# Moving two of five convolution blocks per unit from TensorE to the other engines, with three engines sharing their taps

## The chip, the cores and the metric

One NeuronCore of one Trainium2 chip runs the whole kernel. The metric is the device time of one execution in microseconds; the median of three runs is given. A profile of one execution shows where the time of the engines goes.

## The reference, cut to what matters

The input is `x` of 8 sequences of 4096 tokens with 192 channels, as one list of 32768 tokens. Each of 8 heads (24 channels each) has 7 taps, made positive and normalised by a softmax. A causal convolution along the tokens is followed by two matrix products with an activation between them:

```python
w = softmax(weight)                                     # 8 heads x 7 taps
out[b, s, h] = sum_k w[h, k] * x_pad[b, s + k, h]       # 6 zeros ahead of each sequence
h = out @ w_in                                          # 192 -> 2048
g = h * cos(h)
return g @ w_out                                        # 2048 -> 192
```

## The kernel before, in words

The 32768 tokens are cut into 32 **units** of 1024 tokens. A unit is two **tiles** of 512 tokens; the loop runs over 64 tiles. I call the first tile of a unit the even tile and the second the odd tile.

A tile has eight **h steps** (`mm1`, lines 488 to 504). Step h*j* makes 256 of the 2048 hidden features for 512 tokens with six matmuls, in three pairs: the two matmuls of a pair use the upper and lower 64 rows of the array at once. The result takes two PSUM banks; three such double banks are used in turn, so step j+3 cannot begin before step j has been read out. ScalarE makes `cs = cos(h)` (a Sin, line 510), VectorE multiplies `g = h * cs` (line 514). The second product (`mm2_step`, line 552) of the tile before is spread between the h steps: 64 pairs of matmuls with 192 columns a tile. In the orders, `m9` means nine such pairs. VectorE and ScalarE copy one half of the result each (line 571).

In the middle of a tile's second product the halves of the array change places (`q`). To be sure that no two row halves write one bank at once, the class `Turn` lets a no-operation on SyncE (line 196) wait for the last matmuls ahead of the change, and lets the first matmul after it wait for that no-operation. The convolution does the same between its two halves `c1` and `c2`. SyncE works its queue strictly in order, and all transfers of the steady part are issued from the same queue.

From unit 4 on (`FIRST_RAW`) the convolution is done in two ways. A **conv block** of 112 tokens is done on TensorE with a band matrix (`conv_unit`, line 277: 16 matmuls, eight pairs, for all conv blocks of a unit together), copied by ScalarE into `ct_buf` (line 294) and turned by a transposing DMA (`X` and `x`, line 317). A **raw block** is turned first (`T`, line 345: `rT` holds channels on the partitions and tokens along the row), and its seven taps are multiplied and summed there. ScalarE makes the products of three taps into `pa` (line 356), in two halves of 348 elements; GpSimd makes the other four in one instruction of 2784 elements (line 363), adds the three of ScalarE and sums the rest in three adds (lines 370, 374, 377), giving `ro`. Four DMAs per unit (`U`, line 387) spread `ro` into `cT`, from where `mm1` reads. GpSimd also casts the loaded unit to bfloat16 (`K`, line 211).

The order of everything is written out by hand. `PE_ORDER` has one string for the even and one for the odd tile; it holds TensorE's steps and the points at which the steps of other queues are put into their queues. `ACT_ORDER` gives what ScalarE and VectorE do after the steps: `s3` is cos and product of step h3, `a211` a tap product (tap 2, half 1, put after h1), `Q` and `P` the two copies, `ec2` and `ec1` the copies of the convolution. `K+3` casts the unit three ahead, `L+4` loads the one four ahead, `T+3` turns the raw blocks of the unit three ahead, `R+1` is GpSimd's convolution for the next unit, `U+0` spreads the raw result of the unit at hand, `O` stores.

Before the change a unit has five conv blocks (560 tokens) and four raw blocks of 116 tokens. The even tile's 512 tokens come from conv blocks alone.

Of the kernel before, what the change touches and what calls it, by code (L numbers as in the profile page):

```python
# [16 lines left out]
def kernel(  # L17
# [14 lines left out]
    T = 512  # L32
# [26 lines left out]
    xf = x.rearrange("b s d -> (b s) d")  # L59

# [7 lines left out]
    rT_pool = ctx.enter_context(tc.tile_pool(name="rT", bufs=3))  # L68
# [21 lines left out]
    def load_unit(u, n0=0, n1=UB, queue=nc.sync):  # L90
        if u >= FIRST_RAW:
            x_tiles[u] = xin.tile([128, UB + 1, D], FP32, name="x_f")

            raw = NPB * OP + OR - 128
            for n0, n1, t0, step in ((NPB, NPB + 2, raw, 2 * OR), (NPB + 2, UB + 1, raw + OR, 2 * OR), (0, NPB, OP - 128, OP)):
                rows = xf[u * U + t0 : u * U + t0 + 128, :]
                rows = bass.AP(rows.tensor, rows.offset, [[D, 128], [step * D, n1 - n0], [1, D]])
                queue.dma_start(out=x_tiles[u][:, n0:n1, :], in_=rows)
# [74 lines left out]
    ct_bufs = [consts.tile([128, 2 * NC * NPB + 1, 64], BF16, name="ct_buf%d" % i) for i in range(2)]  # L173
# [95 lines left out]
    def conv_unit(u, banks):  # L269


        ps = banks()
        sides = [slice(0, 64), slice(64, 128)]

        def mm(h, side):
            first, last = h % 4 == 0 and h // 4 == side, h % 4 == 3 and h // 4 != side
            return nc.tensor.matmul(  # L277
                out=ps[h // 4][0:OP, 0 : NPB * 4 * G].rearrange("p (m i r) -> p i m r", m=NC * NPB, i=4)[:, h % 4],
                lhsT=band[sides[side], h, 128 - OP : 128], rhs=xk[u][sides[side], 0 : NC * NPB, R * h : R * (h + 1)],
                start=first, stop=last, skip_group_check=True)  # L280

        for h in range(4):
            ms = mm(h, 0), mm(h + 4, 1)
        turn = Turn()
        turn.mark(*ms)
        yield
        for h in range(4):
            ms = mm(h + 4, 0), mm(h, 1)
            if h == 0:
                turn.wait(*ms)  # L290
        yield
        for b in range(2):
            w0 = 4 * R * b
            nc.scalar.copy(ct_bufs[u % 2][0:OP, 0 : 2 * NC * NPB].rearrange("p (k n) m -> p k n m", k=NC)[:, :, 1 : NPB + 1, w0 : w0 + 4 * R],  # L294
                           ps[b][0:OP, 0 : NPB * 4 * G].rearrange("p (k n w) -> p k n w", k=NC, w=4 * R))
            if b:
                have.update((("conv", u, 0), ("conv", u, 1)))
            yield
# [10 lines left out]
    def turn_unit(u, n0=0, n1=UB + 1, part=0):  # L309
        if u >= FIRST_RAW:  # L310
            assert {("conv", u, 0), ("conv", u, 1)} <= have
            if part == 0:
                cT[u] = cT_pool.tile([128, NC * (UB + 1) * 128], BF16, name="cT")
            else:
                have.update((("whole", u, 0), ("whole", u, 1)))
            to = cT[u][:, 0 : NC * CW].rearrange("p (n s t) -> p s n t", s=2, t=OP)
            nc.sync.dma_start_transpose(out=to[:, part],
                                        in_=ct_bufs[u % 2][0:OP, part : part + 2 * NC * NPB].rearrange("p s m -> p (s m)"))
# [33 lines left out]
    def taps(u, j, half, mul):  # L352
        if u not in pa:
            pa[u] = pa_pool.tile([128, PA, WN, OR], FP32, name="pa")
        part = slice(HALF * half, HALF * (half + 1))
        mul(pa[u][:, j, part], tap_window(u, j)[:, part], tap[:, j : j + 1])  # L356

    raw_prod = consts.tile([128, K - PA, WN, OR], FP32)

    def conv_raw(u):  # L360

        a, p = pa.pop(u), raw_prod
        nc.gpsimd.tensor_tensor(out=p, in0=tap_window(u, PA, K),  # L363
                                in1=tap[:, PA:K].rearrange("p (j a b) -> p j a b", a=1, b=1).to_broadcast([128, K - PA, WN, OR]),
                                op=ALU.mult)
        add = nc.gpsimd.tensor_tensor
        n, done = K - PA, 0
        while done < PA:
            m = min(n, PA - done)
            add(out=p[:, 0:m], in0=p[:, 0:m], in1=a[:, done : done + m], op=ALU.add)  # L370
            done += m
        while n > 2:
            m = n // 2
            add(out=p[:, 0:m], in0=p[:, 0:m], in1=p[:, n - m : n], op=ALU.add)  # L374
            n -= m
        ro[u] = ro_pool.tile([128, WN, OR], BF16, name="ro")
        add(out=ro[u], in0=p[:, 0], in1=p[:, 1], op=ALU.add)  # L377

    def spread_raw(u):

        have.add(("raw", u))
        r = ro.pop(u).rearrange("p (k w) t -> p k (w t)", k=NC)
        for to, t0 in ((0, NPB * OP + OP), (1, NPB * OP)):
            d = cT[u][64 * to : 64 * to + 64, t0 : t0 + (NC - 1) * CW + NRB * OR]
            d = bass.AP(d.tensor, d.offset, [d.ap[0], [CW, NC], [2 * OR, 2], [1, 2 * OR]])
            for v in range(2):
                nc.sync.dma_start(out=d[:, :, v], in_=r[64 * v : 64 * v + 64])

    def mend_edges(u):

# [97 lines left out]
    def mm1(t, j, n0=0, n1=NB):  # L488

        assert ("whole", t // TPU, t % TPU) in have  # L490
        assert t < TPU * FIRST_RAW or t % TPU == 0 or ("raw", t // TPU) in have
        c = cT[t // TPU]
        h = h_pool.tile([128, 2, T], FP32, name="h")
        for k in range(NC):
# [97 lines left out]
    PE_FIRST = ["K1 h0a h0b W0 h1 h2 h3 r h4 w5 d11 w4 h5 d21 W1 c11 X0 m1 h6 m11 h7 L2 c21 D1",  # L592
# [19 lines left out]
    for t in range(NT + 1):  # L612
# [13 lines left out]
        def flush():  # L626
            while act:
# [8 lines left out]
                if k in "PQA":  # L636
                    if 0 <= made < NT - 1:
                        evac(made, int(k != "P"), nc.scalar.copy if k == "A" else None)
                elif k[0] in "ab":
                    if u + 2 in rT:  # L640
                        taps(u + 2, int(k[1]), int(k[2]), nc.scalar.mul if k[0] == "a" else nc.vector.tensor_scalar_mul)
                elif k[0] == "e":
                    next(conv[part_of(k[1:])], None)
                elif k[0] == "s" and t < NT:
                    gcu(t, int(k[1]), h[k[1:2] if k[2:] in "lr" else k[1:]], *HALVES[k[2:]])

        def of_unit(k, v):
# [7 lines left out]
            elif k == "L":  # L655
                load_unit(v)
                if v < FIRST_RAW:
                    load_edges(v)
            else:
                {"K": cast_unit, "D": double_unit, "X": turn_unit, "Y": mend_edges, "T": turn_raw, "R": conv_raw,  # L660
                 "U": spread_raw, "x": lambda u: turn_unit(u, part=1)}[k](v)

        for k in pe.split():
# [22 lines left out]
            elif k[1:] and k[1] != "+":  # L686
                of_unit(k[0], int(k[1]))
            else:
                if u + int(k[2:]) < NU and (k[0] not in "RUx" or u + int(k[2:]) >= FIRST_RAW):
                    of_unit(k[0], u + int(k[2:]))  # L690
            done.add(k)
            flush()
# [33 lines left out]
```

## Time and profile before

| | us |
|---|---|
| median of three runs (705.02 to 705.48) | 705.17 |
| span of the profiled execution | 703.5 |
| what a run has beside that span (705.17 less 703.5) | 1.7 |
| TensorE busy | 697.0 |
| VectorE busy | 642.4 |
| ScalarE busy | 644.4 |
| GpSimd busy | 503.7 |

The profile gives no time of its own for the profiled execution beside its span, so the span is set against the median of the runs. Busy times are unions of instruction spans. Matmuls are pipelined: their recorded spans overlap, and the pace of TensorE is read from the distance between starts. The clock granted to TensorE is 1.00 in every stretch of the steady part. In the rows, L followed by a number is a line of the kernel, `x16` a count, and a time in brackets is idle time with what ended it.

### The profile page before, as it was taken

The page shows a single profiled execution, that of the slowest core. Times are in us where ns is not written, and L with a number is a line of the kernel's source. Part 1 is how long each engine was busy: PE and PEld are TensorE (multiplying, and loading weights), DVE is VectorE, ACT ScalarE, POOL GpSimd, SP SyncE. Part 2 cuts the span into 40 slices and gives each one's busy share as a digit, 9 for nine tenths or more (in the row PEclk, how much of TensorE's full clock was granted, in tenths as well). Part 3 has the DMA queues.
Part 4 walks back from the last instruction along what each step waited for, and adds up shares of the span by engine and source line. Part 5 has one row for each costly group of instructions (what it writes and reads, how often), then busy time and mean ns, then how long its engine had stood idle before and what let it go on. Part 6 is the DMA issues. An engine that isn't in the chain of part 4 may idle for free.

```text
span 703.5 us, 26826 instructions
## 1 busy us (share of the span) xinstructions
PE 697.0 (99%) x11830; PEld 512.8 (73%) x11830; DVE 642.4 (91%) x598; ACT 644.4 (92%) x831; POOL 503.7 (72%) x214
## 2 busy tenths in 40 slices
PE   8999999999999999999999999999999999999997
PEld 4677777777777777777777777777777777777776
DVE  6889999999999999999999999999999999999996
ACT  7889999999999999999999999999999999999875
POOL 6524478977778877778877688877789778799400
PEclk9999999999999999999999999999999999999999
DMA  8964456667667768676656577577665576874331
GB/s 214 234 167 97 120 135 143 138 147 164 138 153 146 131 145 176 134 152 131 147 152 153 150 159 129 140 161 150 143 147 132 145 174 137 153 127 95 92 91 47
DMA packets 228292, 100.09 MB, mean 142 GB/s; under 512 B 156240, under 2 KB 227792, under 8 KB 228176
## 3 DMA queue, kind: packets, MB, share of 16 engines
q1 hardware_dynamic: 227464, 97.40, 62.7%
q8 instruction: 92, 1.51, 0.9%
q0 software_dynamic: 416, 0.79, 0.7%
q14 instruction: 24, 0.20, 0.1%
q10 hardware_dynamic: 296, 0.20, 0.1%
HBM read 31.36 MB, written 25.17 MB: 80 GB/s over the span
## 4 chain that ended last, share of the span: by engine, by line
PE 96%; DMA 1%; DVE 1%; POOL 0%; SPq 0%; ACT 0%; issue 0%; POOLq 0%
PE o_ps L552 48%; PE h L503 46%; PE h L277 2%; DMA wo_f<-in_moe_w_out_dram 1%; PE h L552 0%; SPq L124 0%; PE h L229 0%; DVE band L415 0%; POOL wo L120 0%; POOL mask L159 0%; DVE ct L438 0%; PE o_ps L432 0%; ACT mask L164 0%; DVE diag L404 0%; DVE prod L401 0%
## 5 line engine op out<-in xcount | busy, mean ns | idle before, releaser
L514 DVE TENSOR_TENSOR g<-h,cs 128x1024 bf16<-128x1024 f32 (+1 forms) x513 | 604.9, 1216 | 27.9 <-ACT cs L510 24.5
L510 ACT ACTIVATE cs<-h 128x1024 bf16<-128x1024 f32 (+1 forms) x513 | 511.0, 1021 | 44.0 <-PE h L503 30.6
L552 PEld LDWEIGHTS <-g 64*128 64x128 bf16 x8192 | 354.2, 94 | 102.2 <-issue 1.0
L552 PE MATMUL o_ps<-wo,g 64*128 64x192 bf16 x8128 | 420.6, 243 | 0.1
L503 PE MATMUL h<-cT,w 64*128 64x512 bf16 (+1 forms) x3078 | 407.0, 376 | 0.8 <-DVE g L514 0.4
L503 PEld LDWEIGHTS <-w 64*128 64x128 bf16 x3078 | 147.6, 94 | 75.0 <-issue 1.8
L211 POOL CAST xk<-x_f 128x768 bf16<-128x768 f32 (+1 forms) x56 | 76.4, 1367 | 113.9 <-DMA x_f<-in_x_dram 109.3
L363 POOL TENSOR_TENSOR raw_prod<-rT,tap 128x2784 f32<-128x2784 bf16 x28 | 135.3, 4832 | 0.2
L370 POOL TENSOR_TENSOR raw_prod<-raw_prod,pa 128x2088 f32<-128x2088 f32 x28 | 129.1, 4609 | 2.2
L356 ACT ACTIVATE pa<-rT,tap 128x348 f32<-128x348 bf16 x168 | 94.6, 580 | 0.0
L374 POOL TENSOR_TENSOR raw_prod<-raw_prod 128x1392 f32<-128x1392 f32 x28 | 87.9, 3138 | 2.2
L571 DVE COPY o_sb<-o_ps 128x384 f32<-128x384 f32 x62 | 34.6, 557 | 23.7 <-PE o_ps L552 23.5
L377 POOL TENSOR_TENSOR ro<-raw_prod 128x696 bf16<-128x696 f32 x28 | 46.5, 1660 | 2.2
L294 ACT CAST ct_buf<-h 112x480 bf16<-112x480 f32 x56 | 28.6, 562 | 4.1 <-PE h L277 0.6
L571 ACT COPY o_sb<-o_ps 128x384 f32<-128x384 f32 x64 | 30.8, 482 | 0.1
L277 PE MATMUL h<-xk,band 64*112 64x120 bf16 x448 | 21.2, 213 | 0.0
L277 PEld LDWEIGHTS <-band 64*112 64x112 bf16 x448 | 18.0, 127 | 0.0
L219 POOL CAST x_bf<-x_f 128x768 bf16<-128x768 f32 (+2 forms) x5 | 9.1, 1812 | 7.0 <-DMA x_f<-in_x_dram 6.9
L307 POOL COPY ct<-ct 128x1728 bf16<-128x1728 bf16 x3 | 4.9, 1630 | 8.9 <-ACT ct L239 8.9
L394 POOL COPY cT<-cT 128x144 bf16<-128x144 bf16 x3 | 0.9, 308 | 13.5 <-DMA cT<-ct 13.5
L136 PE MATMUL o_ps<-zero 128*128 128x512 bf16 x21 | 7.2, 492 | 1.3 <-DVE zero L131 1.3
L239 ACT CAST ct<-h 128x432 bf16<-128x432 f32 x12 | 5.9, 530 | 0.4 <-issue 0.4
(66 smaller groups left out, 52.7 us busy)
## 6 DMA issues: line engine op xcount, KB each, us to landing
out_dram<-o_sb SPq DMA_DIRECT2D x63, 384.0 KB, 3.7
x_f<-in_x_dram SPq DMA_DIRECT2D x28, 480.0 KB, 5.5
x_f<-in_x_dram SPq DMA_DIRECT2D x56, 192.0 KB, 2.7
cT<-ro SPq DMA_DIRECT2D x112, 87.0 KB, 2.3
x_f<-in_x_dram SPq DMA_DIRECT2D x4, 384.0 KB, 5.6
wo_f<-in_moe_w_out_dram SPq DMA_DIRECT2D x4, 384.0 KB, 7.9
x_f<-in_x_dram SPq DMA_DIRECT2D x2, 768.0 KB, 5.2
cT<-ct_buf SPq DMA_TRANSPOSE x56, 4.0
```

The lines of the kernel that those rows point to most:

```text
L211: copy(out=xk[u][:, NC * n0 : NC * n1].rearrange("p (k n) m -> p k n m", k=NC), in_=x_tiles[u][:, n0:n1].rearrange("p n (m k) -> p k n m", ...
L277: return nc.tensor.matmul(out=ps[h // 4][0:OP, 0 : NPB * 4 * G].rearrange("p (m i r) -> p i m r", m=NC * NPB, i=4)[:, h % 4], lhsT=band[si ...
L356: mul(pa[u][:, j, part], tap_window(u, j)[:, part], tap[:, j : j + 1])
L363: nc.gpsimd.tensor_tensor(out=p, in0=tap_window(u, PA, K), in1=tap[:, PA:K].rearrange("p (j a b) -> p j a b", a=1, b=1).to_broadcast([128, ...
L370: add(out=p[:, 0:m], in0=p[:, 0:m], in1=a[:, done : done + m], op=ALU.add)
L374: add(out=p[:, 0:m], in0=p[:, 0:m], in1=p[:, n - m : n], op=ALU.add)
L377: add(out=ro[u], in0=p[:, 0], in1=p[:, 1], op=ALU.add)
L503: nc.tensor.matmul(out=h[:, i, n0 * 128 : n1 * 128], lhsT=w[rows, k, j, :], rhs=rhs, start=(k == 0), stop=(k == NC - 1))
L510: nc.scalar.activation(out=cs[:, :, part], in_=h[:, :, part], func=AF.Sin, bias=math.pi / 2.0, scale=1.0)
L514: nc.vector.tensor_tensor(out=g_tiles[t][:, 2 * j : 2 * j + 2, part], in0=h[:, :, part], in1=cs[:, :, part], op=ALU.mult)
L552: ms.append(nc.tensor.matmul(out=o_ps[tt, b, si], lhsT=g_tiles[tt][rows, f, s * 128 : (s + 1) * 128], rhs=wo[rows, f // 2, f % 2, :], star ...
L571: (copy or copies[b])(o_sb[t][:, 2 * b : 2 * b + 2, :].rearrange("p s d -> p (s d)"), o_ps.pop((t, b)))
```

## The change

- Three conv blocks a unit (336 tokens) instead of five; six raw blocks of 115 tokens instead of four of 116. Six times 115 is two more than the 688 tokens left, so the first raw block overlaps the conv blocks by two tokens (`OVER`), which `spread_raw` leaves out. The array `pa` and each tap then have 9 x 115 = 1035 elements a partition instead of 6 x 116 = 696.
- The band matrices are loaded with 128 columns instead of 112; each convolution matmul streams 72 columns instead of 120. The turned buffer keeps ten slots per channel group, so the transposing DMAs keep their size.
- The seven taps of the raw blocks: ScalarE makes the products of two (before three), in parts of 575 and 460 elements. VectorE multiplies one further tap and adds it to ScalarE's first product in one instruction (`tap_on`, a `scalar_tensor_tensor`; two instructions a unit, 575 and 460 elements); both inputs are in SBUF, one bfloat16 and one float32. GpSimd makes four products, now one `tensor_scalar` each (`tap_raw`, `R`), and sums in three adds (`sum_raw`, `S`).
- `R` and `S` run two units ahead (`R` was one ahead), so the raw result is ready a unit earlier; `U+1` spreads it in the odd tile before its unit, since the even tile now reads raw blocks too. `x+1` moves from the odd to the even tile. The pools `rT` go from three buffers to two.
- New steady orders for both tiles, and for tile 5.

```diff
-    NPB, OP = 5, 112
-    NRB = 4
-    OR = (U - NPB * OP) // NRB
+    NPB, OP = 3, 112
+    NRB = 6
+    OR = -(-(U - NPB * OP) // NRB)
+    OVER = NRB * OR - (U - NPB * OP)
     WN = NC * NRB // 2
-    PA = 3
-    HALF = WN // 2
-    CW = 2 * NPB * OP
+    PA, PV = 2, 1
+    SLOTS = 10
+    CW = SLOTS * OP
...
-                lhsT=band[sides[side], h, 128 - OP : 128], rhs=xk[u][sides[side], 0 : NC * NPB, R * h : R * (h + 1)],
+                lhsT=band[sides[side], h, 128 - OP : 256 - OP], rhs=xk[u][sides[side], 0 : NC * NPB, R * h : R * (h + 1)],
...
+    PARTS = {"w": slice(0, WN), "l": slice(0, (WN + 1) // 2), "r": slice((WN + 1) // 2, WN)}
+    def taps(u, j, part):
...
+        nc.scalar.mul(pa[u][:, j, part], tap_window(u, j)[:, part], tap[:, j : j + 1])
+    def tap_on(u, j, part):
+        nc.vector.scalar_tensor_tensor(out=pa[u][:, j, part], in0=tap_window(u, PA + j)[:, part],
+                                       scalar=tap[:, PA + j : PA + j + 1], in1=pa[u][:, j, part], op0=ALU.mult, op1=ALU.add)
+    NG = K - PA - PV
+    def tap_raw(u):
+        p = raw_prod
+        for j in range(NG):
+            nc.gpsimd.tensor_scalar(out=p[:, j], in0=tap_window(u, PA + PV + j), scalar1=tap[:, PA + PV + j : PA + PV + j + 1],
+                                    scalar2=1.0, op0=ALU.mult, op1=ALU.mult)
+    def sum_raw(u):
+        a, p, add = pa.pop(u), raw_prod, nc.gpsimd.tensor_tensor
+        add(out=p[:, 0:PA], in0=p[:, 0:PA], in1=a, op=ALU.add)
+        add(out=p[:, 0:2], in0=p[:, 0:2], in1=p[:, 2:4], op=ALU.add)
         ro[u] = ro_pool.tile([128, WN, OR], BF16, name="ro")
         add(out=ro[u], in0=p[:, 0], in1=p[:, 1], op=ALU.add)
...
-    PE_ORDER = ['m12 h0 m4 h1 K+3 R+1 m5 h2 m7 q h3 U+0 m6 h4 m17 h5 X+1 m9 p h6 h7 O m4', 'm11 h0 m4 h1 m6 h2 m7 q x+1 h3 m5 h4 m7 c1 m8 c2 m3 h5 T+3 L+4 m9 p O h6 h7 m4']
-    ACT_ORDER = ['s0 s1 a211 s2 s3 s4 a014 a114 Q s5 P s6 s7 a007', 's0 s1 s2 a102 s3 a203 s4 Q ec2 ec1 s5 P s6 s7']
+    PE_ORDER = ['m11 h0 m3 h1 X+1 m6 h2 m8 q h3 K+3 m6 h4 m17 h5 m9 p x+1 h6 O h7 m4', 'm9 h0 m4 h1 m6 R+2 m2 h2 m7 q h3 S+2 m5 h4 U+1 m7 c1 m9 c2 m3 h5 T+3 L+4 O m8 p h6 h7 m4']
+    ACT_ORDER = ['s0 s1 s2 a0l2 b0l2 s3 s4 a1l4 Q s5 P s6 s7', 'a0r0 s0 s1 s2 s3 a1r3 b0r3 s4 Q ec2 ec1 s5 P s6 s7']
...
-                 'm11 h0 m4 h1 m6 h2 m7 q x+1 Y3 h3 m5 h4 m7 c1 m8 c2 m3 h5 T+3 L+4 m9 p O h6 h7 m4']
+                 'm11 h0 m4 h1 R+2 m6 h2 m7 q Y3 h3 S+2 m5 h4 m7 c1 m8 c2 m3 h5 T+3 L+4 m9 p O h6 h7 m4']
```

In `ACT_ORDER` a letter `b` now stands for VectorE's tap: `a0l2 b0l2` in the even tile are ScalarE's product of tap 0 and VectorE's addition to it, left part, after h2; `b0r3` is the right part, in the odd tile after h3.

More of the change, by code (lines that the diff above doesn't have):

```diff
@@ L92, in load_unit @@
             x_tiles[u] = xin.tile([128, UB + 1, D], FP32, name="x_f")
-            raw = NPB * OP + OR - 128
-            for n0, n1, t0, step in ((NPB, NPB + 2, raw, 2 * OR), (NPB + 2, UB + 1, raw + OR, 2 * OR), (0, NPB, OP - 128, OP)):
+            raw, half = NPB * OP - OVER + OR - 128, NRB // 2
+            for slots, t0, step in ((slice(NPB, UB + 1, 2), raw, OR), (slice(NPB + 1, UB + 1, 2), raw + half * OR, OR),
+                                    (slice(0, NPB), OP - 128, OP)):
                 rows = xf[u * U + t0 : u * U + t0 + 128, :]
-                rows = bass.AP(rows.tensor, rows.offset, [[D, 128], [step * D, n1 - n0], [1, D]])
-                queue.dma_start(out=x_tiles[u][:, n0:n1, :], in_=rows)
+                rows = bass.AP(rows.tensor, rows.offset, [[D, 128], [step * D, half if slots.step else NPB], [1, D]])
+                queue.dma_start(out=x_tiles[u][:, slots, :], in_=rows)
             return
@@ L172 @@
     wn = consts.tile([128, HQ, K], BF16)
-    ct_bufs = [consts.tile([128, 2 * NC * NPB + 1, 64], BF16, name="ct_buf%d" % i) for i in range(2)]
+    ct_bufs = [consts.tile([128, NC * SLOTS + 1, 64], BF16, name="ct_buf%d" % i) for i in range(2)]
     wmax = consts.tile([128, HQ, 1], FP32)
@@ L350, in tap_window @@
         return w if j1 is None else bass.AP(w.tensor, w.offset, [w.ap[0], [1, j1 - j0], *w.ap[1:]])
-    def taps(u, j, half, mul):
+    PARTS = {"w": slice(0, WN), "l": slice(0, (WN + 1) // 2), "r": slice((WN + 1) // 2, WN)}
+    def taps(u, j, part):
         if u not in pa:
             pa[u] = pa_pool.tile([128, PA, WN, OR], FP32, name="pa")
[L355 to L375, printed above, removed]
+        nc.scalar.mul(pa[u][:, j, part], tap_window(u, j)[:, part], tap[:, j : j + 1])
[3 more added lines that the diff above has]
+    NG = K - PA - PV
+    raw_prod = consts.tile([128, NG, WN, OR], FP32)
+    def tap_raw(u):
[7 more added lines that the diff above has]
+        add(out=p[:, 0:2], in0=p[:, 0:2], in1=p[:, 2:4], op=ALU.add)
         ro[u] = ro_pool.tile([128, WN, OR], BF16, name="ro")
@@ L382, in spread_raw @@
         r = ro.pop(u).rearrange("p (k w) t -> p k (w t)", k=NC)
+        run = NRB // 2 * OR
         for to, t0 in ((0, NPB * OP + OP), (1, NPB * OP)):
[L384 to L385 removed]
             for v in range(2):
[L387 removed]
+                skip = 0 if v else OVER
+                d = cT[u][64 * to : 64 * to + 64, t0 : t0 + (NC - 1) * CW + 2 * run - OVER]
+                d = bass.AP(d.tensor, d.offset + v * (run - OVER), [d.ap[0], [CW, NC], [1, run - skip]])
+                nc.sync.dma_start(out=d, in_=r[64 * v : 64 * v + 64, :, skip:])
     def mend_edges(u):
@@ L490, in mm1 @@
         assert ("whole", t // TPU, t % TPU) in have
-        assert t < TPU * FIRST_RAW or t % TPU == 0 or ("raw", t // TPU) in have
+        assert t < TPU * FIRST_RAW or ("raw", t // TPU) in have
         c = cT[t // TPU]
@@ L688 @@
             else:
-                if u + int(k[2:]) < NU and (k[0] not in "RUx" or u + int(k[2:]) >= FIRST_RAW):
+                if u + int(k[2:]) < NU and (k[0] not in "RSUx" or u + int(k[2:]) >= FIRST_RAW):
                     of_unit(k[0], u + int(k[2:]))
```

12 lines of the change are left out of this document (6 added, 6 removed).

## The prediction

> **What bounds the kernel now.** I read the page's engine shares and its chain first, then one unit's stretch among the windows, then the groups by form, and last the timeline of single steps.
>
> ```profile
> span 703.5 us, 26826 instructions
> PE 697.0 (99%) x11830; PEld 512.8 (73%) x11830; DVE 642.4 (91%) x598; ACT 644.4 (92%) x831; POOL 503.7 (72%) x214
> ...
> PE 96%; DMA 1%; DVE 1%; POOL 0%; SPq 0%; ACT 0%; issue 0%; POOLq 0%
> ```
>
> ```profile
> 360.39:381.73 21.34, 21.34 (x373) 15.65 (x371) 19.86 (x19) 20.11 (x26) 17.61 (x8) 1.00 0.61 147
> ```
>
> TensorE carries 96% of the chain, and in the unit from 360.39 it has no idle time: 21.34 us busy of 21.34, at a granted clock of 1.00. A busy TensorE need not be one at its pace, so I look at the distance between starts (columns: start, duration with overlap, what).
>
> ```profile
> 357.21 0.81 PE L503 MATMUL h<-cT,w 64*128 64x512 bf16 x6
> 357.86 0.74 PE L552 MATMUL o_ps<-wo,g 64*128 64x192 bf16 x14
> 358.43 0.81 PE L503 MATMUL h<-cT,w 64*128 64x512 bf16 x6
> ...
> 371.18 0.37 PE L277 MATMUL h<-xk,band 64*112 64x120 bf16 x8
> 371.39 0.82 PE L552 MATMUL o_ps<-wo,g 64*128 64x192 bf16 x16
> ```
>
> Three pairs of 512 columns take 0.65 us (357.21 to 357.86), seven pairs of 192 take 0.57 (81 ns a pair), four convolution pairs of 120 take 0.21 (52 ns). A unit has 16 h steps, 128 second-product pairs and 8 convolution pairs: 10.4 + 10.4 + 0.4 = 21.2 us, the period within rounding. TensorE streams without a gap. Only less work on it can make the kernel faster, and any wait that reaches it costs its full length.
>
> **How close the others are.** VectorE and ScalarE are in use for 19.9 and 20.1 us of the 21.34. Successive instructions overlap a little, so their pace is again read from starts:
>
> ```profile
> 357.08 2.35 DVE L514 TENSOR_TENSOR g<-h,cs 128x1024 bf16<-128x1024 f32 x2 [0.26 <-ACT cs L510]
> ```
>
> ```profile
> 359.44 3.49 DVE L514 TENSOR_TENSOR g<-h,cs 128x1024 bf16<-128x1024 f32 x3
> ```
>
> ```profile
> 352.75 0.56 DVE L571 COPY o_sb<-o_ps 128x384 f32<-128x384 f32 x1 [0.51 <-PE o_ps L552]
> 353.23 3.59 DVE L514 TENSOR_TENSOR g<-h,cs 128x1024 bf16<-128x1024 f32 x3
> ...
> 361.35 1.05 ACT L356 ACTIVATE pa<-rT,tap 128x348 f32<-128x348 bf16 x2
> ...
> 363.87 1.94 ACT L510 ACTIVATE cs<-h 128x1024 bf16<-128x1024 f32 x2
> ```
>
> ```profile
> L514 DVE TENSOR_TENSOR g<-h,cs 128x1024 bf16<-128x1024 f32 x511 | 603.6, 1218 | 27.1 <-ACT cs L510 23.7
> L510 ACT ACTIVATE cs<-h 128x1024 bf16<-128x1024 f32 x511 | 509.9, 1023 | 43.7 <-PE h L503 30.3 <-DVE g L514 0.6
> L363 POOL TENSOR_TENSOR raw_prod<-rT,tap 128x2784 f32<-128x2784 bf16 x28 | 135.3, 4832 | 0.2
> L370 POOL TENSOR_TENSOR raw_prod<-raw_prod,pa 128x2088 f32<-128x2088 f32 x28 | 129.1, 4609 | 2.2
> L374 POOL TENSOR_TENSOR raw_prod<-raw_prod 128x1392 f32<-128x1392 f32 x28 | 87.9, 3138 | 2.2
> L377 POOL TENSOR_TENSOR ro<-raw_prod 128x696 bf16<-128x696 f32 x28 | 46.5, 1660 | 2.2
> L356 ACT ACTIVATE pa<-rT,tap 128x348 f32<-128x348 bf16 x168 | 94.6, 580 | 0.0
> L211 POOL CAST xk<-x_f 128x960 bf16<-128x960 f32 x28 | 42.2, 1506 | 43.6 <-DMA x_f<-in_x_dram 38.9 <-ACT pa L356 4.4 <-ACT cs L510 0.3
> L211 POOL CAST xk<-x_f 128x768 bf16<-128x768 f32 x28 | 34.4, 1228 | 70.4 <-DMA x_f<-in_x_dram 70.4
> L552 PEld LDWEIGHTS <-g 64*128 64x128 bf16 x8192 | 354.2, 94 | 102.2 <-issue 1.0
> L277 PEld LDWEIGHTS <-band 64*112 64x112 bf16 x448 | 18.0, 127 | 0.0
> L120 POOL CAST wo<-wo_f 128x1536 bf16<-128x1536 f32 x2 | 2.9, 1470 | 3.1 <-DMA wo_f<-in_moe_w_out_dram 3.1
> ```
>
> Two products g take 2.35 us, one 1.22, so the next begins 1.13 after the first; a copy of 384 takes the engine 0.48 (352.75 to 353.23). Likewise cos takes ScalarE 0.92, a tap of 348 elements 0.47. The ring is also tight: g of the step at 355.17 ends at 357.08 + 1.22 = 358.30, and the step that takes its banks over begins at 358.43, 0.13 us later.
>
> **TensorE.** From 192 to 120 columns a pair goes from 81 to 52 ns, 0.40 ns a column. With 72 columns a pair takes 52 - 48 x 0.40 = 33 ns; 8 pairs and 28 units make 224 x 19.5 ns = **4.4 us less**. The other bound is nothing, if loading the band sets the pace. The loads get shorter (127 ns for 112 columns, 94 for 128), so I take the whole.
>
> **ScalarE** loses two instructions a unit for about the same elements (2070 instead of 2088), and its two convolution copies shrink by 192 elements each; it gets looser and costs nothing.
>
> **VectorE.** No row shows a `scalar_tensor_tensor`. From 0.48 us for 384 and 1.13 for 1024 elements: 1.02 ns an element and 0.09 fixed, so 575 and 460 take 0.67 and 0.56 us. A unit then holds 16 x 1.13 + 2 x 0.48 + 1.23 = 20.3 of 21.2 us. It fits on average; what matters is how far the step behind it is put off. I follow both places.
>
> Odd tile, from the start of h3: matmuls 0.81 and 0.04 to ScalarE, cos 1.02 and 0.03 to VectorE, g3 1.13, the tap 0.56, g4 1.22: 4.81 us until the banks of h4 are free. TensorE reaches h6, which takes them, after two steps more of h (h3, h4, h5 at 0.65), 5 + 7 + 9 + 3 + 8 pairs of 81 ns and four convolution pairs twice at 33 ns: 1.95 + 2.59 + 0.26 = 4.80. Nothing is left over.
>
> Even tile, from h2: its g begins after 2.2 us now (the step at 357.21, its g at 359.44, behind two others), then g2 1.13, tap 0.67, g3 1.13, g4 1.13, copy 0.48, g5 1.13, g6 1.22: 9.1 us, against 7 steps of h (4.55) and 57 pairs (4.62) until step h1 of the odd tile, which takes the banks of g6: 9.2. About 0.1 us is left.
>
> So the orders leave room for the tap's own length and for nothing on top. Each further tenth of a microsecond of VectorE at these places is a stall of TensorE, 2.8 us over 28 units.
>
> **GpSimd beside VectorE's taps.** The adds: 2.11 ns an element (4609 less 3138 over 696) and 0.20 fixed give 4.57, 4.57 and 2.38 us. The four products lie between the cast of contiguous data (1470 ns for 1536: 0.96 ns an element, 1.0 us each) and the old product (4832 for 2784: 1.74, 1.8 each); one tensor input is nearer to the cast, so 1.1 each. With 2.73 for the casts a unit takes 18.7 us of 21.2. At the other bound it takes 21.4, 0.2 too much; over 28 units that is 6 us, about the lead there is (the sums end some 8 us into the next unit, `U+1` spreads them 14 us into it). So GpSimd costs nothing by its own length.
>
> VectorE has so far read only one operand from SBUF at a time in the steady part (h is in PSUM). The new tap reads two while GpSimd reads SBUF. The one place where both work on SBUF together is the start:
>
> ```profile
> L415 DVE CAST band<-diag x7: 188/251/293, 6.0 to 7.6; 32x76 bf16<-32x76 f32 x7
> L415 POOL CAST band<-diag x7: 238/243/245, 6.1 to 7.9; 32x76 bf16<-32x76 f32 x7
> ```
>
> The same cast of VectorE takes 188 ns at the least and 251 in the middle, up to 293, while GpSimd's stay at 243: VectorE loses 60 to 105 ns next to an instruction of 243 ns. For the tap that gives from 0.1 us up to the rest of a GpSimd add. Where is GpSimd? Its sums wait for the odd tile's tap, so they begin with its end, when the products (4.4 us) are done and GpSimd is idle; the odd tap loses little, 0.1. The even tap comes 9.2 us later (the odd tap ends 17.4 us into the unit of 21.2, the even one begins 5.4 us into the next, by the same steps), and the first two adds take 9.1 with two gaps of 0.08 (2.2 us over 28): it meets the end of the second add. The bounds are 0.06 us and the whole third add behind it; I take 0.25, near the row. Less the 0.1 left over, the stalls are 0.15 + 0.1 = 0.25 a unit: **7 us more**.
>
> The Trainium skill, page "SBUF — State Buffer", section "Who interferes with whom", says that a VectorE instruction with two SBUF inputs contends with a GpSimd instruction that reads SBUF, and that the second to issue is blocked until the first is done. The 60 to 105 ns agree that something is held up, not how long. By that rule the tap would wait for a whole add; its price is the third rival's.
>
> **SyncE.** `U+1` now stands between the mark of `q` and the mark of `c1`, and TensorE's `c2` waits for the second mark.
>
> ```profile
> 358.77 3.40 SPq L387 DMA_DIRECT2D cT<-ro  x4
> 362.27 1.56 SPq L317 DMA_TRANSPOSE cT<-ct_buf  x1
> ```
>
> ```profile
> L387 SPq DMA_DIRECT2D cT<-ro x112: 596/612/1620, 102.7 to 681.0; - x112
> ```
>
> ```profile
> SPq L196 <- PE h L277: 25.4, 26, 2.5
> ```
>
> The third row shows SyncE waiting for these marks. The four issues begin 0.34 us after h3 (358.77 against 358.43) and take 4 x 0.612 and gaps, 2.6 us, or 3.4 as in the first row. TensorE is at `c2` 0.65 x 2 + 21 pairs + 4 x 33 ns = 3.1 us after h3. With 2.6 the mark comes just in time, with 3.4 about 0.65 late. All 28 units late would be 18 us, none is nothing; the median is the short one, so I take one unit in six: **3 us more**. `X+1` now stands ahead of the even tile's mark, but its 1.56 us begin when the queue is free, and q comes 3.3 us into the tile; `x+1`, `T` and `L` have longer. These cost nothing.
>
> **Sum.** 703.5 - 4.4 + 7 + 3 = 709.1 of span, and 1.7 around it (705.17 less 703.5): **711 us**.
>
> **The rivals.** What this kernel's measurement tells from no change is 0.2%, 1.4 us: 703.8 to 706.6 counts as the same.
>
> - *Nothing is held up.* The tap runs at its own length and the marks come in time: 705.2 - 4.4 + 0 to 3 = 700.8 to 703.8, about 702. For it: the orders fit the bare lengths to the tenth. Against it: the L415 row. 0.32.
> - *The parts cancel* between 703.8 and 706.6: 0.10.
> - *The tap waits for whole instructions of GpSimd* (slower). In the even tile it stays behind the third add as well, 0.25 + 2.4 us, less 0.1: 28 x 2.55 = 71 us. That gives 705.2 - 4.4 + 71 = 772, and 735 if half of the third add is waited for (28 x 1.1 = 31, with SyncE's 3). It decides as soon as the hold-up passes 0.1 + 0.16 us a unit, room and gain together. From 735 on: 0.18.
> - *The band load keeps its pace at 52 ns*, and the gain is not there: 715 by my sum; inside the forecast.
>
> My forecast, short hold-ups that reach TensorE, has 0.40 and reaches from 706.6 to 735. Slower is 0.40 + 0.18 = 0.58, faster 0.32, the same 0.10. The range 701 to 752 leaves out a tenth above and little below; the forecast's own is 706.6 to 735.
>
> **What would show it.** Right: convolution pairs 33 ns apart; even-tile taps well above 0.76 us (0.67 and the 0.09 by which 1.22 passes 1.13) where an add runs beside them, odd ones near 0.65; idle PE before L503 ended by VectorE. Wrong: no idle PE in a unit and a period of 21.18 (nothing held up), taps of 2 us and more or VectorE waiting in front of them (third rival), or PE idle before L277 throughout, which makes SyncE's term the main one.

## The result, and the profile after

The changed kernel takes 752.56 us (median of four runs, 752.46 to 752.75) against 705.23 for the kernel before on the same chip: a ratio of 1.0672, interval 1.0657 to 1.0687. It is slower, as forecast, but by 47 us and not by 6; it lies just outside the range, whose upper end was 752. The span went from 703.5 to 751.0 us.

The head of the page after, with the engines' busy times and the shares of the chain:

```profile
span 751.0 us, 26948 instructions
PE 706.4 (94%) x11828; PEld 522.4 (70%) x11830; DVE 713.8 (95%) x654; ACT 633.2 (84%) x775; POOL 544.7 (73%) x298
...
PE 60%; DVE 25%; issue 6%; ACT 4%; SPq 3%; DMA 1%; POOL 0%; POOLq 0%
```

VectorE's share of the chain went from 1% to 25%, so TensorE no longer sets the end alone. One unit among the windows after (stretch, length, then busy time of PE, PEld, DVE, ACT and POOL, granted clock, DMA share, GB/s):

```profile
385.81:408.89 23.08, 21.65 (x372) 16.25 (x368) 22.62 (x21) 19.73 (x25) 18.39 (x10) 1.00 0.73 156
```

A unit takes 23.08 us instead of 21.34, with the clock at 1.00 as before; 28 times the difference is 48.7 us, near the 47.5 by which the span grew. VectorE is busy for 22.62 of the 23.08, which looks like an engine with too much to do. The groups by form (line, engine, operation, out<-in, count; busy, mean ns; idle time in front) show that it is not:

```profile
L362 DVE SCALAR_TENSOR_TENSOR pa<-rT,tap,pa 128x575 f32<-128x575 bf16 x28 | 69.9, 2497 | 0.0
L362 DVE SCALAR_TENSOR_TENSOR pa<-rT,tap,pa 128x460 f32<-128x460 bf16 x28 | 19.3, 689 | 0.0
L378 POOL TENSOR_TENSOR raw_prod<-raw_prod,pa 128x2070 f32<-128x2070 f32 x28 | 128.2, 4577 | 129.2 <-DVE pa L362 129.2
L379 POOL TENSOR_TENSOR raw_prod<-raw_prod 128x2070 f32<-128x2070 f32 x28 | 107.8, 3850 | 2.2
L381 POOL TENSOR_TENSOR ro<-raw_prod 128x1035 bf16<-128x1035 f32 x28 | 66.7, 2383 | 2.2
L372 POOL TENSOR_SCALAR raw_prod<-rT,tap 128x1035 f32<-128x1035 bf16 x112 | 126.9, 1153 | 0.1
```

The tap of 460 elements, in the odd tile, takes 689 ns; the tap of 575 in the even tile takes 2497 ns in the mean. The second of GpSimd's two adds of the same size takes 3850 ns and the first 4577. The timelines of VectorE and GpSimd around one even tap show what it is beside (start, duration, engine, line):

```profile
396.52 0.69 DVE L362 SCALAR_TENSOR_TENSOR pa<-rT,tap,pa 128x460 f32<-128x460 bf16 x1
...
406.25 2.72 DVE L362 SCALAR_TENSOR_TENSOR pa<-rT,tap,pa 128x575 f32<-128x575 bf16 x1
408.89 1.21 DVE L520 TENSOR_TENSOR g<-h,cs 128x1024 bf16<-128x1024 f32 x1
```

```profile
388.35 4.50 POOL L372 TENSOR_SCALAR raw_prod<-rT,tap 128x1035 f32<-128x1035 bf16 x4
397.39 4.58 POOL L378 TENSOR_TENSOR raw_prod<-raw_prod,pa 128x2070 f32<-128x2070 f32 x1 [4.54 <-DVE pa L362]
402.05 3.85 POOL L379 TENSOR_TENSOR raw_prod<-raw_prod 128x2070 f32<-128x2070 f32 x1
405.98 2.38 POOL L381 TENSOR_TENSOR ro<-raw_prod 128x1035 bf16<-128x1035 f32 x1
408.31 3.17 POOL L213 CAST xk<-x_f 128x1152 bf16<-128x1152 f32 x2
```

GpSimd is done with its four products at 392.85 and idle for 4.54 us until the odd tap is there; then it adds without a pause. The third add starts at 405.98, the tap 0.27 us later at 406.25, and the tap ends at 408.97. The third add ends at 408.36. From there to the tap's end are 0.61 us. A tap of its size that nothing holds up takes 0.81 us (first experiment), so it is let in some 0.2 us before the add's recorded end. VectorE counts as busy for the 1.9 us in which it is held up. TensorE then waits for the banks:

```profile
410.16 0.82 PE L509 MATMUL h<-cT,w 64*128 64x512 bf16 x6 [1.12 <-DVE g L520]
```

```profile
PE h L509 <- DVE g L520: 34.8, 55, 1.1
PE h L279 <- SPq L198: 3.7, 6, 1.1
```

Over 28 units the even taps last (2497 - 808) x 28 = 47.3 us longer than the bare 808 ns, TensorE waits for SyncE's marks 3.7 us (second row), and its own work is 28 x 0.16 = 4.5 us less, as shown below; this makes 46.5 us, against 47.5 us of added span. Only 34.8 us of the hold-ups stand as idle time of TensorE (first row): its busy time grew from 697.0 to 706.4 us although its work shrank, so the recorded spans of its matmuls cover a part of the waits.

### The profile page after: what moved, and what is told of

Same layout as the page of the kernel before. It is cut to its first block, busy times and chain, and to the rows that moved or that the text cites. A ratio compares the mean times of both kernels' runs of the same rounds, so it can differ in the third digit from the quotient of the medians.

```text
span 751.0 us, 26948 instructions
## 1 busy us (share of the span) xinstructions
PE 706.4 (94%) x11828; PEld 522.4 (70%) x11830; DVE 713.8 (95%) x654; ACT 633.2 (84%) x775; POOL 544.7 (73%) x298
## 4 chain that ended last, share of the span: by engine, by line
PE 60%; DVE 25%; issue 6%; ACT 4%; SPq 3%; DMA 1%; POOL 0%; POOLq 0%
PE h L509 30%; PE o_ps L558 29%; DVE g L520 20%; DVE pa L362 4%; ACT cs L516 4%; SPq L393 3%; DMA wo_f<-in_moe_w_out_dram 1%; PE h L279 1%; PE h L558 0%; SPq L126 0%; PE h L231 0%; POOL wo L122 0%; PE o_ps L438 0%; ACT L182 0%; ACT x_bf L221 0%
## 5 line engine op out<-in xcount | busy, mean ns | idle before, releaser
L509 PE MATMUL h<-cT,w 64*128 64x512 bf16 (+1 forms) x3078 | 415.8, 376 | 35.0 <-DVE g L520 34.8
L378 POOL TENSOR_TENSOR raw_prod<-raw_prod,pa 128x2070 f32<-128x2070 f32 x28 | 128.2, 4577 | 129.2 <-DVE pa L362 129.2
L372 POOL TENSOR_SCALAR raw_prod<-rT,tap 128x1035 f32<-128x1035 bf16 x112 | 126.9, 1153 | 0.1
L379 POOL TENSOR_TENSOR raw_prod<-raw_prod 128x2070 f32<-128x2070 f32 x28 | 107.8, 3850 | 2.2
L362 DVE SCALAR_TENSOR_TENSOR pa<-rT,tap,pa 128x575 f32<-128x575 bf16 (+1 forms) x56 | 89.2, 1593 | 0.0
L213 POOL CAST xk<-x_f 128x1152 bf16<-128x1152 f32 (+1 forms) x56 | 87.6, 1594 | 0.0
L359 ACT ACTIVATE pa<-rT,tap 128x575 f32<-128x575 bf16 (+1 forms) x112 | 81.3, 726 | 0.0
L381 POOL TENSOR_TENSOR ro<-raw_prod 128x1035 bf16<-128x1035 f32 x28 | 66.7, 2383 | 2.2
L296 ACT CAST ct_buf<-h 112x288 bf16<-112x288 f32 x56 | 19.6, 402 | 8.7 <-PE h L279 5.9
L279 PE MATMUL h<-xk,band 64*128 64x72 bf16 x448 | 17.3, 194 | 3.7 <-SPq L198 3.7
L279 PEld LDWEIGHTS <-band 64*128 64x128 bf16 x448 | 13.7, 95 | 5.2 <-SPq L198 5.1
```

Source lines behind the costliest of these rows:

```text
L213: copy(out=xk[u][:, NC * n0 : NC * n1].rearrange("p (k n) m -> p k n m", k=NC), in_=x_tiles[u][:, n0:n1].rearrange("p n (m k) -> p k n m", ...
L359: nc.scalar.mul(pa[u][:, j, part], tap_window(u, j)[:, part], tap[:, j : j + 1])
L362: nc.vector.scalar_tensor_tensor(out=pa[u][:, j, part], in0=tap_window(u, PA + j)[:, part], scalar=tap[:, PA + j : PA + j + 1], in1=pa[u][ ...
L372: nc.gpsimd.tensor_scalar(out=p[:, j], in0=tap_window(u, PA + PV + j), scalar1=tap[:, PA + PV + j : PA + PV + j + 1], scalar2=1.0, op0=ALU ...
L378: add(out=p[:, 0:PA], in0=p[:, 0:PA], in1=a, op=ALU.add)
L379: add(out=p[:, 0:2], in0=p[:, 0:2], in1=p[:, 2:4], op=ALU.add)
```

## The experiments

Theory A: a VectorE instruction with two SBUF inputs waits until the GpSimd instruction that is running is done, so what it costs hangs on where in that instruction it comes. Rival B: it is slow by its size or shape, or by VectorE being full. Rival C: the loss comes from the rest of the change and not from the tap. A unit's period, where given, is the distance between the starts of the convolution step in successive units. The orders are shown for `ACT_ORDER`; moves of queue points in `PE_ORDER` are told in words. Each run has the kernel before beside it on the same chip; the second time given is that kernel's, and the brackets hold the ratio and its interval.

**The parts change places.**

```diff
-    ACT_ORDER = ['s0 s1 s2 a0l2 b0l2 s3 s4 a1l4 Q s5 P s6 s7', 'a0r0 s0 s1 s2 s3 a1r3 b0r3 s4 Q ec2 ec1 s5 P s6 s7']
+    ACT_ORDER = ['s0 s1 s2 a0r2 b0r2 s3 s4 a1l4 Q s5 P s6 s7', 'a0l0 s0 s1 s2 s3 a1r3 b0l3 s4 Q ec2 ec1 s5 P s6 s7']
```

> The two parts of VectorE's tap change places: the 460-element part in the even tile after h2, the 575-element part in the odd tile after h3. Theory A (the tap waits for the GpSimd instruction that runs when it arrives): length goes with the place. Even tap (460) 2.3 to 2.8 us, odd tap (575) about 0.80 us (0.689 + 115 x 1.02 ns), time within 3 us of the changed kernel's 752.6. Theory B (the 575-element form is slow by itself): length goes with the size. Even tap 0.69, odd tap about 2.5 us.

752.44 us against 705.05 (1.0672, 1.0656 to 1.0688). Its groups by form:

```profile
L362 DVE SCALAR_TENSOR_TENSOR pa<-rT,tap,pa 128x460 f32<-128x460 bf16 x28 | 67.2, 2399 | 0.0
L362 DVE SCALAR_TENSOR_TENSOR pa<-rT,tap,pa 128x575 f32<-128x575 bf16 x28 | 22.6, 808 | 0.0
```

The long one is now the shorter part. The length goes with the place, not with the size.

**No VectorE tap.** Both `b` entries leave `ACT_ORDER`; the raw blocks then lack one of their seven taps.

> Left out: VectorE's tap, both parts (one of seven taps is missing from the raw blocks). Everything else is as in the changed kernel. Theory A (the hold-up of the even tap is the whole loss): TensorE streams again, period 21.18 us a unit, 705.2 - 4.4 = 701, up to 704 with SyncE's late marks. Theory C (the loss comes from the rest of the change: the spread ahead of c1, two rT buffers, GpSimd's longer sums, the new orders): 715 or more, idle TensorE remains.

705.05 us against 705.05 (1.0, 0.9991 to 1.0009), 1 us above the expected bracket. The 47 us are gone. Undisturbed units take 21.18 us, 0.16 less than before; five take 21.5 to 22.5. There TensorE waits in front of the convolution for SyncE, whose four issues of `U+1` took longer (timelines of TensorE and of SyncE's queue, and the wait's row):

```profile
222.31 0.30 PE L279 MATMUL h<-xk,band 64*128 64x72 bf16 x8 [0.70 <-SPq L198]
```

```profile
218.67 3.52 SPq L393 DMA_DIRECT2D cT<-ro  x4
```

```profile
PE h L279 <- SPq L198: 3.2, 5, 1.2
```

This kernel shows what the lighter TensorE is worth, 28 x 0.16 = 4.5 us, and that the late marks take most of it back: the five units are 4.0 us over 21.18 together.

**Both taps in the odd tile.** `b0l2` goes out of the even tile, `b0l4` comes in behind `s4` of the odd one, and the sums start after h4 there.

```diff
+    ACT_ORDER = ['s0 s1 s2 a0l2 s3 s4 a1l4 Q s5 P s6 s7', 'a0r0 s0 s1 s2 s3 a1r3 b0r3 s4 b0l4 Q ec2 ec1 s5 P s6 s7']
```

> Nothing is left out. Both parts of VectorE's tap go to the odd tile, after h3 and after h4, where GpSimd waits for them and does nothing; GpSimd's sums start after the second. Theory A: both taps at bare length, 0.69 and 0.80 us, no GpSimd instruction beside them, 701 to 705 in time. Theory B: the 575-element part still takes about 2.5 us, now after h4, and the time stays above 740. Theory C: time as without the tap, above 715.

708.18 us against 705.05 (1.0042, 1.0025 to 1.0059): the same work on the same engines is 44 us faster than in the changed kernel, because the sums wait for both taps and none runs beside them. The longest tap takes 811 ns. The time is 3 us above the expected one: the period is 21.30, so the ring loses 0.12 us a unit in the fuller odd tile, and the marks come late as in the run before.

**The same with the marks out of the way.** `x+1` goes behind q, after h3, of the even tile and `U+1` after h0 of the odd one, well ahead of any mark that TensorE needs.

> The kernel of e3 (both parts of the tap in the odd tile, nothing left out) with only x+1 and U+1 moved as in e6. If the place of the spread ahead of the mark of c1 makes the late units: every period 21.3, none of 21.4 to 22.6, about 4 us less than e3's 708.2, 703.5 to 704.8. If not: 708, late units as before.

704.40 us against 705.17 (0.9989, 0.9981 to 0.9998), with 21.3 us in every unit. By the ratios it is 0.5% below the run before, some 3.7 us: that is what the late marks cost in a kernel without hold-ups.

```profile
L362 DVE SCALAR_TENSOR_TENSOR pa<-rT,tap,pa 128x575 f32<-128x575 bf16 x28 | 22.6, 809 | 0.0
```

**The third add in two instructions.**

```diff
-        add(out=ro[u], in0=p[:, 0], in1=p[:, 1], op=ALU.add)
+        for part in (PARTS['l'], PARTS['r']):
+            add(out=ro[u][:, part], in0=p[:, 0, part], in1=p[:, 1, part], op=ALU.add)
```

> GpSimd's third add (1035 elements, 2.38 us) is made in two instructions (575 and 460 elements, by its rate about 1.4 and 1.15 us). The tap arrives 0.28 us after its start. Theory A with the wait ending at the end of the running instruction: even tap held about 1.1 us instead of 2.1, its length about 1.7 us, time 705.2 - 4.4 + 28 x about 0.9 = 722 to 730. Theory A2 (the tap waits until GpSimd's queue of ready work is done, not for one instruction): no gain, 750 to 755. Theory B: no gain.

726.39 us against 705.05 (1.0307, 1.0291 to 1.0322). VectorE's timeline, then GpSimd's:

```profile
349.12 1.73 DVE L362 SCALAR_TENSOR_TENSOR pa<-rT,tap,pa 128x575 f32<-128x575 bf16 x1
```

```profile
348.83 3.04 POOL L382 TENSOR_TENSOR ro<-raw_prod 128x575 bf16<-128x575 f32 x2
```

The tap comes 0.29 us after the start of the first part and is let in at the seam, between two instructions of GpSimd that follow each other: 0.92 us of hold-up instead of 1.91, period 22.10. It waits for an instruction to end, not for GpSimd to be idle.

**A longer GpSimd.** One more instruction of 0.58 us (times 1) between the first and the second add, so that the second add ends later.

```diff
+        nc.gpsimd.tensor_scalar(out=p[:, 3, PARTS['r']], in0=p[:, 3, PARTS['r']], scalar1=1.0, scalar2=1.0, op0=ALU.mult, op1=ALU.mult)
```

> One GpSimd instruction is added between its first and second add (460 elements of an array multiplied by 1 in place, about 0.55 us); the result is the same. Theory A with the phase as the traces show it: the even tap arrives 8.86 us after the sums begin, 0.28 us behind the start of the third add; with 0.55 us more in front of it, it arrives about 0.27 us before the end of the second add and is held only that long. Even tap about 1.1 us instead of 2.7, time 705.2 - 4.3 + 4 (SyncE's late marks) + 28 x 0.2 = about 710. Theory A3 (what counts is how much GpSimd does, not when): slower than the changed kernel, 752 or more. Theory B (the form is slow): 752.

715.18 us against 705.1 (1.0143, 1.0127 to 1.016): more work makes the kernel 37 us faster. A usual unit, VectorE and GpSimd:

```profile
342.99 0.81 DVE L362 SCALAR_TENSOR_TENSOR pa<-rT,tap,pa 128x575 f32<-128x575 bf16 x1
```

```profile
338.67 0.58 POOL L379 TENSOR_SCALAR raw_prod<-raw_prod 128x460 f32<-128x460 f32 x1
339.34 3.85 POOL L380 TENSOR_TENSOR raw_prod<-raw_prod 128x2070 f32<-128x2070 f32 x1
343.27 2.78 POOL L382 TENSOR_TENSOR ro<-raw_prod 128x1035 bf16<-128x1035 f32 x1
```

The second add now ends at 343.19, and the tap, at 342.99, gets in ahead of the third add and runs at its own 0.81; the period is 21.27. The third add pays instead: 2.78 us, where it took 2.38. A hold-up of 0.27 was expected, and none is recorded. In four units a late mark puts the tap off, to the start of the third add or into it, and it takes 1.92 to 3.02 us. The longest comes at the start and waits for the whole add:

```profile
407.05 3.02 DVE L362 SCALAR_TENSOR_TENSOR pa<-rT,tap,pa 128x575 f32<-128x575 bf16 x1
```

In the usual unit the tap comes 0.28 us ahead of the third add's recorded start, in the late one 0.02 ahead of it (407.07, next row): 0.26 us lie between 0.81 and 3.02.

```profile
407.07 2.38 POOL L382 TENSOR_TENSOR ro<-raw_prod 128x1035 bf16<-128x1035 f32 x1
```

Seven of the unit periods are above 21.4 us, by 8.7 us over 21.27 together; so the time lies above the forecast 710 although the usual tap is not held.

**The tap earlier, within the second add.** The left part goes from h2 to h1 of the even tile: `s0 s1 a0l1 b0l1 s2`.

> The changed kernel with one edit: the left part of the tap (and ScalarE's product ahead of it) after h1 instead of h2 of the even tile. The tap then arrives 1.14 us earlier, about 7.7 us after GpSimd's sums begin and 0.8 us before its second add ends. Theory A (wait for the end of the running instruction, whichever it is): held 0.8 us, even part about 1.6 us long and ending about 0.6 us after the second add's end, time 717 to 725. If the third add alone held the tap, or the length were its own: 0.81 us and below 706, or 2.7 us and 752.

721.55 us against 705.17 (1.0223, 1.0207 to 1.0239).

```profile
L362 DVE SCALAR_TENSOR_TENSOR pa<-rT,tap,pa 128x575 f32<-128x575 bf16 x28 | 39.6, 1413 | 0.0
```

A usual tap, on VectorE, and the second add beside it, on GpSimd:

```profile
345.31 1.40 DVE L362 SCALAR_TENSOR_TENSOR pa<-rT,tap,pa 128x575 f32<-128x575 bf16 x1
```

```profile
342.24 3.85 POOL L379 TENSOR_TENSOR raw_prod<-raw_prod 128x2070 f32<-128x2070 f32 x1
```

The usual tap takes 1.37 to 1.40 us: it is held for some 0.57 us, to the end of the second add (346.09), and the period is 21.75. Expected were taps of 1.6.

**One SBUF input.** The tap multiplies only; ScalarE's product is overwritten instead of added to.

```diff
-        nc.vector.scalar_tensor_tensor(out=pa[u][:, j, part], in0=tap_window(u, PA + j)[:, part],
-                                       scalar=tap[:, PA + j : PA + j + 1], in1=pa[u][:, j, part], op0=ALU.mult, op1=ALU.add)
+        nc.vector.tensor_scalar_mul(pa[u][:, j, part], tap_window(u, PA + j)[:, part], tap[:, PA + j : PA + j + 1])
```

> Left out: the addition in VectorE's tap; it only multiplies (one SBUF tensor input, output over ScalarE's product of tap 0), at the same two places. Theory A with the second input as the reason: even part not held, at most 0.8 us, time 700 to 706. Theory A with any SBUF work of VectorE that takes the port it shares with GpSimd as the reason: still held by the third add, even part about 2.3 to 2.7 us, time 745 to 755.

705.32 us against 705.1 (1.0003, 0.9992 to 1.0013). VectorE, then GpSimd:

```profile
338.88 0.80 DVE L362 TENSOR_SCALAR pa<-rT,tap 128x575 f32<-128x575 bf16 x1
```

```profile
338.45 2.39 POOL L380 TENSOR_TENSOR ro<-raw_prod 128x1035 bf16<-128x1035 f32 x1
```

At the same place, 0.43 us into the third add, with the same length, an instruction with one SBUF input isn't held at all, nor is the add. The edit changes the kind of instruction too, but two inputs alone do not make the wait: the product g reads one input from PSUM and one from SBUF, and the longest of the changed kernel's 513 took 1226 ns, as in the kernel before, with GpSimd busy for 73% of the span. So the wait comes with the second SBUF input. The Trainium skill, page "SBUF — State Buffer", section "Who interferes with whom", says that a VectorE instruction with at most one SBUF input, outside the modes that use two ports, does not contend with GpSimd; the 0.80 us agree.

**The first two adds change places**, with `x+1` and `U+1` moved as above. The add without `pa` needs no tap and can run while GpSimd waits for the odd one.

```diff
-        add(out=p[:, 0:PA], in0=p[:, 0:PA], in1=a, op=ALU.add)
         add(out=p[:, 0:2], in0=p[:, 0:2], in1=p[:, 2:4], op=ALU.add)
+        add(out=p[:, 0:PA], in0=p[:, 0:PA], in1=a, op=ALU.add)
```

> The first two of GpSimd's three adds change places: the one that reads raw_prod alone comes first (it needs no tap and fits into the 4.5 us in which GpSimd waited for the odd tap), the one with pa second; x+1 goes after q of the even tile and U+1 after h0 of the odd one, as in the run without late marks. From the odd tap on GpSimd then has 4.58 + 2.38 and two gaps of 0.08 = 7.1 us of adds instead of 11.0, and the even tap comes 8.86 us after them, at the end of the cast of 1152 elements (1.76 us, 7.1 to 8.9), the next cast being 0.9 long. Theory A (the tap waits for the rest of the GpSimd instruction that is running): held 0 to 0.1, period 21.18 to 21.3, 700.5 to 704.5 us; if it comes just behind the start of the second cast, held 0.9, period near 22.0, about 722. Rival B (hold-up belongs to the length and place of VectorE's tap): 2.5 us taps and 750 as in the changed kernel. On the adds' lengths: if the shorter 3.85 us goes with the operands (both of one array), the first add is now 3.85 and the second 4.58; if it goes with the position behind another add, the first is 4.58 and the second 3.85.

716.28 us against 705.14 (1.0157, 1.0143 to 1.0172), with a usual period of 21.74 to 21.80: between the two expected cases, nearer to the held one. VectorE, then GpSimd:

```profile
365.42 1.40 DVE L362 SCALAR_TENSOR_TENSOR pa<-rT,tap,pa 128x575 f32<-128x575 bf16 x1
```

```profile
363.52 2.69 POOL L213 CAST xk<-x_f 128x1152 bf16<-128x1152 f32 x2
366.18 5.00 POOL L372 TENSOR_SCALAR raw_prod<-rT,tap 128x1035 f32<-128x1035 bf16 x4
371.27 3.85 POOL L378 TENSOR_TENSOR raw_prod<-raw_prod 128x2070 f32<-128x2070 f32 x1
378.31 4.58 POOL L379 TENSOR_TENSOR raw_prod<-raw_prod,pa 128x2070 f32<-128x2070 f32 x1 [3.20 <-DVE pa L362]
```

The tap now meets the second cast of the pair, just behind its start, is held for 0.59 us to its end, and the products behind it are longer in turn (four take 5.00 instead of 4.50). So it isn't only the adds: casts hold it too. And the 3.85 us go with the operands, not with the position.

**One tap of full width in the odd tile.** `b0w4` behind `s4` in place of the two parts, with the sums after h4; `x+1` and `U+1` moved.

> Nothing is left out. VectorE's tap is one instruction of 1035 elements after h4 of the odd tile, where GpSimd waits for it; x+1 goes behind q of the even tile and U+1 behind h0 of the odd tile, so the four issues of the spread no longer stand ahead of the mark of c1. Theory A with SyncE's marks as the second loss: tap about 1.2 us, no GpSimd instruction beside it, period 21.18 to 21.3 in every unit and none of 21.5 to 22.5, 701 to 703. If the late marks come from something else than the place of the spread: 704 to 706.

710.42 us against 705.1 (1.0075, 1.0062 to 1.0088), above both expected brackets. The row of the tap:

```profile
L362 DVE SCALAR_TENSOR_TENSOR pa<-rT,tap,pa x28: 1285/1286/1289, 74.4 to 655.4; 128x1035 f32<-128x1035 bf16 x28
```

The tap is never held and costs VectorE less than two parts (1286 against 808 + 689 ns), but put on at one place it takes the ring 0.34 us a unit: all periods are 21.52. No unit is late, so the moved points do what they should. Less work, put at one place, is worse here than more work at two (704.40).

**The tap on ScalarE.** ScalarE makes a third product instead, GpSimd's first add takes three arrays, and the store's pool goes to two buffers to make room; `x+1` and `U+1` moved.

```diff
-    PA, PV = 2, 1
+    PA, PV = 3, 0
...
-    opool = ctx.enter_context(tc.tile_pool(name="o", bufs=3))
+    opool = ctx.enter_context(tc.tile_pool(name="o", bufs=2))
...
+    ACT_ORDER = ['s0 s1 s2 a0l2 s3 s4 a1l4 a2l4 Q s5 P s6 s7', 'a0r0 s0 s1 a2r1 s2 s3 a1r3 s4 Q ec2 ec1 s5 P s6 s7']
```

> Nothing is left out. ScalarE makes VectorE's tap as a third product; GpSimd's first add takes three products (3105 elements, about 6.8 us); the store has two buffers instead of three to make room; x+1 and U+1 placed as in e6. VectorE reads no two SBUF operands at any time. GpSimd then has about 20.3 us a unit. Theory A: period 21.18, 701 to 702. If GpSimd's length or ScalarE's load decides: units of 21.3 and more, 704 or above.

701.32 us against 705.1 (0.9947, 0.9933 to 0.9961): 0.5% below the kernel before and the shortest time of all runs here. A unit of it:

```profile
300.00:321.18 21.18, 21.18 (x371) 16.34 (x369) 19.96 (x19) 20.15 (x28) 20.35 (x11) 1.00 0.76 161
```

TensorE is at its pace again in every unit, with GpSimd at 20.35 of 21.18 us, and nothing in it reads two SBUF inputs on VectorE.

## Why the prediction was wrong

**TensorE's 4.4 us were right.** In the timeline after, four convolution pairs take 0.12 us here and 0.13 in the mean, 32 ns a pair (33 predicted):

```profile
395.75 0.31 PE L279 MATMUL h<-xk,band 64*128 64x72 bf16 x8
395.87 0.92 PE L558 MATMUL o_ps<-wo,g 64*128 64x192 bf16 x18
```

Where nothing is held up the period is 21.18, as forecast. The rival that the load of the band keeps the pace at 52 ns is out.

**The bare taps and the room were right.** 0.81 and 0.69 us recorded, against 0.76 and 0.65 with overlap. The ring's room was put at 0.1 us in the even tile: typical taps after are 1.91 us over the bare one, the period 1.90 over 21.18, and 1.81 over the 21.27 of the run with the longer GpSimd, whose usual units hold no tap up. So at most 0.1 us was left over, and the hold-up reached TensorE nearly in full, as the step said.

**The odd tap** was to lose 0.1 and loses nothing (689 ns in every run that has this part there with both inputs): GpSimd has nothing left to do and waits for it, 129.2 us in all in front of L378.

**The step that failed is the even tap's hold-up: 0.25 us taken, 1.9 measured.** It was worked out from two times. The tap's was right: it was to come 9.2 us after the odd one's end and comes 9.04 after it (397.21 to 406.25). The other, the end of the second add, was wrong: both adds of 2070 elements were given 4.57 us, from one slope through three adds of before. The first took 4.577. The second took 3.85, so the third add had already begun when the tap came. With 4.57 the second would have ended at 406.62, 0.37 us after the tap came. In the run with the tap after h1 a tap that came 0.78 us ahead of that end took 1.40, and in the longer GpSimd one that came 0.49 ahead (at 451.69) took 1.10: they were held 0.59 and 0.29. So this one would have been held some 0.2, the size that was forecast. A term wrong by 0.72 us put the tap behind the border of another instruction; there the cost jumps by the length of that one. The experiments on both sides show this jump: 37 us less with 0.58 us more of GpSimd, 26 less when the third add is cut in two.

**The third rival named the mechanism**, the wait for whole instructions, and had 0.18. The measured 752.56 lies between its two prices, 735 for half of the third add and 772 for all of it. The 772 was 20 too high: it added the end of the second add to the whole third, while the tap waits only for the rest of the add that is running. With 1.9 us a unit and 0.16 gained it would have given 705.2 + 28 x 1.74 = 754. The choice of 0.25 between the bounds rested on the L415 row, where VectorE lost 60 to 105 ns; but an instruction of 243 ns can hold nothing up for longer than it lasts, so that row could not tell how long a hold-up can be. Nor is it shown that the row is the same wait: its casts read one SBUF input, and the run with one SBUF input shows no hold-up. What lengthened them stays open. The rule of the Trainium skill that the prediction set beside that row (page "SBUF — State Buffer", section "Who interferes with whom" and its summary of rules: with two SBUF inputs against a GpSimd instruction that reads SBUF, the second to issue is blocked until the first is done) agrees with the runs, in both directions: VectorE's tap is held by a running add or cast, and GpSimd's add is longer when the tap came first (2.78 instead of 2.38 us).

**SyncE's 3 us** were right in size and did not count. TensorE waits 3.7 us for the marks after, in 6 units of 28 where one in six was taken; without hold-ups that costs some 4 us (the runs with both taps in the odd tile, with and without the moved points). In the changed kernel late units are as long as the others, 23.06 to 23.10 us: a late mark puts the tap off, it comes later into the same third add, and is held for that much less. Six of its taps came 0.64 to 1.46 us into that add; the latest, with the add beside it:

```profile
268.96 1.53 DVE L362 SCALAR_TENSOR_TENSOR pa<-rT,tap,pa 128x575 f32<-128x575 bf16 x1
```

```profile
267.50 2.38 POOL L381 TENSOR_TENSOR ro<-raw_prod 128x1035 bf16<-128x1035 f32 x1
```

It took 1.53 us instead of 2.72 and ended 0.61 us behind the add, as the usual tap does. Both waits end with the add. Moving `x+1` and `U+1` in the changed kernel itself was not tried.

**What stays open** is why the add of two slices of one array takes 3.85 us and the one with `pa` 4.58 for the same count; the change of places shows that it goes with the operands, and no run tells alignment, distance or array apart. In the kernel before, the add of two slices of `raw_prod` was not quicker by the element (3138 ns for 1392).

## What to carry to other kernels

When a wait ends with an instruction of another engine, its cost is no smooth function: work out where in that instruction the waiter comes, and if the distance to its border is smaller than the error of the terms, price both sides of the border instead of taking a value between. Before an operation is moved to VectorE, count its SBUF inputs and look at what GpSimd does at that time; a place where GpSimd itself waits for the result was safe here (0.69 and 0.81 us every time). A tightly filled engine is judged by where its work is put, not by its sum: the one-piece tap was shorter and cost more.

## What the hardware showed that was not expected

- VectorE's `scalar_tensor_tensor` with two SBUF inputs waits to the end of GpSimd's running instruction (add or cast: 0.81 becomes 2.72 us with 2.1 us of the add left, 1.40 beside the rest of a cast) and counts as busy meanwhile; a `tensor_scalar` with one SBUF input runs beside it (0.80).
- It gets in between two GpSimd instructions that follow each other (1.73 us beside the add in two parts), and the GpSimd instruction behind it is then longer by 0.4 to 0.5 us (2.78 for 2.38; four products 5.00 for 4.50).
- GpSimd's adds of 2070 float32 elements took 3.85 or 4.58 us, by their operands.
